# Rows of a few gradient stores moved between DMA engines, in an attention kernel with one query per head

## The chip, the cores and the metric

The kernel runs on one core of a Trainium2 chip. The metric is the time of one execution on the device in microseconds (us). Before the change the median of seven runs is 1286.94 us (1286.24 to 1287.81).

A core has five engines with instruction streams of their own: PE (matrix products), DVE and ACT (elementwise work), POOL, and SP. Here POOL and SP mainly issue DMAs, which 16 DMA engines carry out between the chip's memory (HBM) and the on-chip memory of 128 partitions.

## The reference

For 2 x 32 heads, each with one query row q of 128 numbers and 8192 keys k and values v, all in bf16, it computes attention and its gradients for a given gradient of the output:

```python
scale = q.shape[-1] ** -0.5
scores = jnp.einsum("bhqd,bhkd->bhqk", q, k) * scale
p = _softmax(scores, axis=-1)
out = jnp.einsum("bhqk,bhkd->bhqd", p, v)
_out0, _vjp = jax.vjp(_f, q, k, v)
_grads = _vjp(grad_out)          # dq, dk, dv
```

dk and dv are as large as k and v: 2 MB per head each. With one query row each of them is an outer product: dk is a column of 8192 weights times q, dv a column of 8192 weights times the output's gradient. So 268 MB are read and 268 MB written, and little is computed on each byte.

## The kernel before

The 64 heads are worked on one after the other. A head's k (or v) is one tile of 128 partitions x 64 x 128 numbers, 16 KB in each partition; partition p holds 64 consecutive rows of the sequence, so a partition of the tile is one contiguous run of 16 KB in HBM. Below, "row" means such a partition, and "dv 52" the store of dv of head 52. Twelve tiles (`NTILE`) are held, six heads' worth.

The main loop (`for g in range`) goes through steps of a quarter of a tile (16 of its 64 blocks), eight (`SL`) for a head, and several heads are in it at once, each in another stage: `transpose_chunk` (PE transposes 16 blocks, L184, ACT copies them out, L186), `score_chunk` (PE, L195), the maximum, `expo` and the sums, `acc` (PE sums p v and dS k, L339), and last `outer` (DVE, L394), which overwrites the chunk of the head's own k or v tile with dk or dv. The call of `outer` for the last chunk of a tile also issues its store. `outer` runs v first, then k, so the stores come in the order dv 0, dk 0, dv 1, dk 1 and so on.

A load of head i+6 goes to a tile that head i has left: `slot_of` gives k of head i+6 the tile of v of head i, and v of head i+6 the tile of k of head i. So the load of k of head 58 has to wait until all of dv 52 has landed in HBM, and the load of k of head 61 until all of dv 55 has.

What sets the order of the DMAs:
- `load_eng` is SP: it issues all loads (L98) in the order of the program, each as one DMA of 128 rows. SP also issues the last head's stores, in quarters (L412), and the two small outputs (L489).
- `store_eng` is POOL: it issues the stores (L412, 119 of them) as one DMA of 128 rows each. At the start it also loads 6 rows of q (`FIRST`, L110), behind an instruction (L108) that resets the cursor by which POOL's DMAs are given to DMA engines; the other 58 rows of q are loaded by SP (L114).
- `by_rows` (L87) issues one store as several DMAs, each of some consecutive rows. With `max_dma_last_dim` a row then goes as two runs of 4096 numbers (8 KB). For dk of the heads in `SPREAD` (5, 14, 23, 32, 41, 50, 59) it makes two DMAs, of 126 and of 2 rows.
- `pin` keeps each of these instructions at its place in its engine's program.

The tile framework adds the waits. Each queue's DMAs use eight completion semaphores in turn, so a DMA also waits for the one eight before it on its queue.

Of the kernel before, what the change touches and what calls it, by code (L numbers as in the profile page):

```python
# [17 lines left out]
NG = 2  # L18
NTILE = 12
FIRST = 6  # L20
SPREAD = range(5, 64, 9)


@with_exitstack
def kernel(
# [12 lines left out]
    B, H, Sq, D = q.shape  # L38
    Sk = k.shape[2]
    P = nc.NUM_PARTITIONS  # L40
# [3 lines left out]
    NT = Sk // P  # L44
# [5 lines left out]
    load_eng = nc.sync  # L50
    store_eng = nc.gpsimd
    pin = tc.keep_in_program_order
# [30 lines left out]
    def by_rows(eng, dst, src, rows):  # L83

        p = 0
        for m in rows:
            pin(eng.dma_start(out=dst[p : p + m], in_=src[p : p + m], max_dma_last_dim=NT * D))  # L87
            p += m
# [15 lines left out]
    for w, a in enumerate((q, grad_out)):  # L104
        rows = a.rearrange("b h s d -> (b h s) d")
        r0 = FIRST if w == 0 else 0
        if r0:
# [3 lines left out]
                    out=qd_nat[:r0, w, :], in_=rows[:r0], max_dma_last_dim=D  # L111
# [276 lines left out]
    def outer(i, w, c, ends):  # L388

        h = heads[i]  # L390
        n0 = c * CH
        shape = [P, CH, D // 2, 2]
        pin(
            nc.vector.tensor_tensor(  # L394
                out=h.tile[w][:, n0 : n0 + CH, :].rearrange("p n (e t) -> p n e t", t=2),
                in0=h.qb[w][:]
                .rearrange("p (e t) -> p e t", t=2)
                .unsqueeze(1)
                .to_broadcast(shape),
                in1=h.pair[w][:, n0 : n0 + CH, :].unsqueeze(2).to_broadcast(shape),  # L400
                op=ALU.mult,
            )
        )
        if c + 1 in ends:
            at = ends.index(c + 1)
            b0, b1 = (ends[at - 1] if at else 0) * CH, (c + 1) * CH
            dst = (dv_v if w else dk_v)[i]
            if w == 0 and i in SPREAD:
                by_rows(store_eng, dst, h.tile[w], (P - 2, 2))
            else:  # L410
                eng = load_eng if len(ends) > 1 else store_eng
                pin(eng.dma_start(out=dst[:, b0:b1, :], in_=h.tile[w][:, b0:b1, :]))  # L412
# [10 lines left out]
    for g in range(SL * BH + O0 + NCH + 4 - SL):  # L423
# [15 lines left out]
        if x := within(O1):  # L439
            outer(x[0], 1, x[1], last if x[0] == BH - 1 else whole)  # L440
        if x := within(O0):
            outer(x[0], 0, x[1], last if x[0] == BH - 1 else whole)
        ev = None
        if g < SL * BH:
            i, r = divmod(g, SL)
# [74 lines left out]
```

## Time and profile before

| | |
|---|---|
| median of seven runs | 1286.94 us (1286.24 to 1287.81) |
| the profiled execution: its time | 1286.09 us |
| the profiled execution: span from first to last instruction | 1284.3 us |
| PE, ACT, DVE, POOL busy | 88%, 76%, 73%, 6% of the span |
| HBM read and written | 268.47 MB each, 418 GB/s over the span |
| stores by POOL in one DMA | 119, 66.1 us from issue to landing |
| stores by POOL with `by_rows` | 7 of 126 rows and 7 of 2 rows, 69.6 us |
| loads by SP of a whole tile | 127, 21.2 us from issue to landing |

The profile is of one execution on the chip, and times in it are us from the start of the span. The page gives each engine's busy time, then the span in 40 slices: the line "DMA" has the mean busy share of the 16 DMA engines in each slice in tenths (9 is 90% or more), "GB/s" what they moved. A third part lists the DMA queues: q1 holds what SP issued, q0 what POOL issued, q8 and q14 fetches of instructions; each has its count of packets, MB, and the share of 16 engines' span that its packets took. Other views used: busy times by stretches of the span, an engine's instructions in order of time, and the waits ("A <- B" means that A stood idle until B was done; SPq is SP's queue). Beneath the page lies the trace, which also holds every DMA packet with queue, start, duration and size.

### The profile page before, as it was taken

Reading aid. Unit: us, or ns where it says so; the run is one execution under the profiler, and the core shown is the slowest. Engines: PE = TensorE matmul, PEld = TensorE weight load, DVE = VectorE, ACT = ScalarE, POOL = GpSimd, SP = SyncE. Lnnn points to the kernel's source line nnn. Section 1 sums busy time; section 2 is a strip of 40 time slices with the busy share of each in tenths; the row PEclk is TensorE's granted clock in tenths of the full one; section 3 lists DMA queues with packets and bytes.
Section 4 is the critical chain, followed back from the end, with each engine's and each line's share of the span. In section 5 each row is a group of like instructions: output and inputs, shape, how many; then the busy total and the mean of one; then the engine's idle time right before and its main releaser. Section 6 shows DMA issues by size and latency. Waiting matters only on the chain.

```text
span 1284.3 us, 42575 instructions
## 1 busy us (share of the span) xinstructions
PE 1133.1 (88%) x19268; PEld 860.5 (67%) x19268; DVE 936.4 (73%) x2122; ACT 975.7 (76%) x641; POOL 75.3 (6%) x142
## 2 busy tenths in 40 slices
PE   6999999989898988988889998899888888989880
PEld 5777777666676666766666776677666666667650
DVE  2888888777687777767776776767777777667781
ACT  6888888777787877877777887778777778777750
POOL 0000000000000000000000000000000000000000
PEclk9999999999999999999998998989999999999885
DMA  9999999999999999999999999999999999999996
GB/s 388 425 425 426 427 426 429 427 426 428 426 428 428 427 427 427 416 427 429 428 427 427 425 428 429 427 426 424 427 427 428 428 422 424 428 428 426 421 395 251
DMA packets 39986, 539.68 MB, mean 420 GB/s; under 512 B 5116, under 2 KB 5116, under 8 KB 6396
## 3 DMA queue, kind: packets, MB, share of 16 engines
q1 hardware_dynamic: 20172, 272.70, 49.9%
q0 software_dynamic: 19632, 264.25, 48.8%
q8 instruction: 150, 2.46, 0.7%
q14 instruction: 32, 0.26, 0.0%
HBM read 268.47 MB, written 268.47 MB: 418 GB/s over the span
## 4 chain that ended last, share of the span: by engine, by line
DMA 38%; another core or an unknown queue 30%; PE 17%; DVE 6%; issue 4%; ACT 1%; SPq 1%; POOL 0%; POOLq 0%; DVEq 0%; ACTq 0%
DMA kvt<-in_v_dram 19%; DMA kvt<-in_k_dram 12%; PE tp L184 8%; DMA out_dram<-kvt 7%; PE acc L339 4%; DVE kvt L394 3%; PE sw L195 2%; PE dpw L195 2%; DVE sel L362 1%; ACT ev L186 1%; SPq L98 1%; DMA qd_nat<-in_q_dram 1%; PE dpw L282 0%; DVE sel L356 0%
## 5 line engine op out<-in xcount | busy, mean ns | idle before, releaser
L186 ACT COPY ev<-tp 128x2048 bf16<-128x2048 bf16 x512 | 954.9, 1866 | 265.4 <-PE tp L184 254.5
L184 PE MATMUL tp<-ident_bf,kvt 128*128 128x128 bf16 x8192 | 560.4, 223 | 90.9 <-DMA kvt<-in_v_dram 72.9
L394 DVE TENSOR_TENSOR kvt<-qb,pair 128x2048 bf16<-128x2048 bf16 x512 | 621.6, 1215 | 0.2
L184 PEld LDWEIGHTS <-kvt 128*128 128x128 bf16 x8192 | 491.2, 101 | 97.8 <-DMA kvt<-in_v_dram 76.8
L195 PEld LDWEIGHTS <-ev 128*128 128x128 bf16 x8192 | 243.0, 96 | 209.5 <-issue 153.8
L339 PE MATMUL acc<-kvt,dS_pad 128*64 128x512 bf16 x1024 | 169.9, 415 | 0.9 <-DVE dqT L379 0.9
L339 PE MATMUL acc<-kvt,E_pad 128*64 128x512 bf16 x1024 | 160.5, 394 | 0.0
L195 PE MATMUL dpw<-qdT,ev 128*128 128x1 bf16 x4096 | 140.7, 164 | 16.6 <-DVE qb L177 15.8
L362 DVE SCALAR_TENSOR_TENSOR sel<-acc,diag,sel 128x128 f32<-128x128 f32 x384 | 134.7, 351 | 13.6
L195 PE MATMUL sw<-qdT,ev 128*128 128x1 bf16 x4096 | 142.0, 164 | 1.3 <-ACT ev L186 1.3
L412 POOL DMA_DIRECT2D out_dram<-kvt x119 | 64.0, 537 | 1088.5 <-DVE kvt L394 959.2
L207 DVE TENSOR_REDUCE mp<-sw 128x1 f32<-128x64 f32 x64 | 14.4, 225 | 154.4 <-PE sw L195 154.4
L339 PEld LDWEIGHTS <-dS_pad 128*64 128x64 bf16 x1024 | 37.8, 111 | 25.1 <-issue 6.3
L247 DVE CAST E_pad<-E_f 128x64 bf16<-128x64 f32 x64 | 12.5, 196 | 56.4 <-ACT E_f L238 56.4
L339 PEld LDWEIGHTS <-E_pad 128*64 128x64 bf16 x1024 | 36.4, 108 | 21.3 <-issue 0.7
L376 PE MATMUL acc<-ones,sel 128*128 128x1 f32 x256 | 43.4, 239 | 6.2 <-DVE sel L362 6.2
L282 PE MATMUL dpw<-ld,ones 128*128 128x1 f32 x256 | 46.3, 250 | 0.1
L253 DVE CUSTOM_DVE_ANT_0 junk<-E_f,dpw 128x64 bf16<-128x64 f32 x64 | 14.2, 221 | 41.5 <-PE dpw L195 41.5
L356 DVE TENSOR_SCALAR sel<-acc,diag 128x128 f32<-128x128 f32 x128 | 44.1, 345 | 0.0
L376 PEld LDWEIGHTS acc<-ones,sel 128*128 128x128 f32 x256 | 39.2, 193 | 7.3 <-DVE sel L362 7.3
L177 DVE CAST qb<-dpw 128x128 bf16<-128x128 f32 x128 | 35.5, 278 | 6.0 <-PE dpw L168 6.0
L282 PEld LDWEIGHTS dpw<-ld,ones 128*128 128x128 f32 x256 | 38.2, 188 | 0.5 <-DVE ld L253 0.5
(44 smaller groups left out, 313.5 us busy)
## 6 DMA issues: line engine op xcount, KB each, us to landing
out_dram<-kvt POOLq DMA_DIRECT2D x119, 2048.0 KB, 66.2
kvt<-in_v_dram SPq DMA_DIRECT2D x64, 2048.0 KB, 21.2
kvt<-in_k_dram SPq DMA_DIRECT2D x63, 2048.0 KB, 21.2
out_dram<-kvt POOLq DMA_DIRECT2D x7, 2016.0 KB, 69.3
out_dram<-kvt SPq DMA_DIRECT2D x8, 512.0 KB, 24.2
kvt<-in_k_dram SPq DMA_DIRECT2D x2, 512.0 KB, 4.4
kvt<-in_k_dram SPq DMA_DIRECT2D x1, 1024.0 KB, 7.0
out_dram<-kvt POOLq DMA_DIRECT2D x7, 32.0 KB, 69.8
```

What stands on the lines that cost most here:

```text
L177: pin(nc.vector.tensor_copy(out=h.qb[w][:], in_=h.qbp))
L184: pin(nc.tensor.transpose(tp[:, t, :], src[:, c * CH + t, :], ident_bf[:]))
L186: pin(nc.scalar.copy(out=ev[:], in_=tp[:]))
L195: nc.tensor.matmul(dst[:, c * CH + t : c * CH + t + 1], lhsT=ev[:, t, :], rhs=qdT[:, w, i : i + 1], start=True, stop=True,)
L207: pin(nc.vector.reduce_max(out=h.mp[:], in_=h.s, axis=AX.X))
L282: nc.tensor.matmul(out, lhsT=ones[:].to_broadcast([P, P]), rhs=col, start=True, stop=True)
L339: nc.tensor.matmul(h.acc[w][g : g + CW, :], lhsT=wts[:, n0 : n0 + CW], rhs=rows[:, n0 : n0 + QT, :].rearrange("p n d -> p (n d)"), start=( ...
L356: nc.vector.tensor_scalar(out=h.sel[:], in0=block, scalar1=diag[:, 0:1], scalar2=None, op0=ALU.mult)
L362: nc.vector.scalar_tensor_tensor(out=h.sel[:], in0=block, scalar=diag[:, b : b + 1], in1=h.sel[:], op0=ALU.mult, op1=ALU.add,)
L376: nc.tensor.matmul(h.acc[w][:, 0:1], lhsT=h.sel[:], rhs=ones[:], start=True, stop=True)
L394: nc.vector.tensor_tensor(out=h.tile[w][:, n0 : n0 + CH, :].rearrange("p n (e t) -> p n e t", t=2), in0=h.qb[w][:] .rearrange("p (e t) -> ...
L412: pin(eng.dma_start(out=dst[:, b0:b1, :], in_=h.tile[w][:, b0:b1, :]))
```

## The change

`SPREAD` now ends at 50, so dk 59 is stored like any other head. The stores dv 52 and dv 55 are cut by rows: dv 52 into 9, 95 and 22 rows issued by POOL and the last 2 rows issued by SP; dv 55 into 95 and 33 rows issued by POOL.

```diff
-SPREAD = range(5, 64, 9)
+SHIFT = (52, 55)
+SPREAD = range(5, 52, 9)
...
             dst = (dv_v if w else dk_v)[i]
-            if w == 0 and i in SPREAD:
+            if w == 1 and i == SHIFT[0]:
+                by_rows(store_eng, dst, h.tile[w], (9, 95, 22))
+                pin(load_eng.dma_start(out=dst[P - 2 :], in_=h.tile[w][P - 2 :], max_dma_last_dim=NT * D))
+            elif w == 1 and i in SHIFT:
+                by_rows(store_eng, dst, h.tile[w], (95, 33))
+            elif w == 0 and i in SPREAD:
                 by_rows(store_eng, dst, h.tile[w], (P - 2, 2))
             else:
                 eng = load_eng if len(ends) > 1 else store_eng
```

In SP's program the new store of 2 rows stands behind the load of v of head 57 and ahead of the load of k of head 58. Lines behind the change move by one (`by_rows` is L88) or by six (the stores are L418, loads stay in one line, L99).

## The prediction

> **What bounds the kernel now.** I read the page from the top: busy shares, then the slices.
>
> ```profile
> PE 1133.1 (88%) x19268; PEld 860.5 (67%) x19268; DVE 936.4 (73%) x2122; ACT 975.7 (76%) x641; POOL 75.3 (6%) x142
> ...
> DMA  9999999999999999999999999999999999999996
> GB/s 388 425 425 426 427 426 429 427 426 428 426 428 428 427 427 427 416 427 429 428 427 427 425 428 429 427 426 424 427 427 428 428 422 424 428 428 426 421 395 251
> ...
> q1 hardware_dynamic: 20172, 272.70, 49.9%
> q0 software_dynamic: 19632, 264.25, 48.8%
> q8 instruction: 150, 2.46, 0.7%
> q14 instruction: 32, 0.26, 0.0%
> ```
>
> No compute engine is full; the 16 DMA engines are, in every slice but the last. Loads run on q1, POOL's stores on q0, instruction fetches on q8 and q14. So the tail decides. The view of stretches shows it (busy time of each engine, then granted clock, DMA share, GB/s):
>
> ```profile
> 1246.00:1258.00 12.00, 5.93 (x25) 2.41 (x21) 11.24 (x20) 0.00 (x0) 0.00 (x0) 0.50 1.01 419
> 1258.00:1262.00 4.00, 0.44 (x2) 0.17 (x2) 0.57 (x3) 0.00 (x0) 0.00 (x0) 0.50 0.91 375
> 1262.00:1265.00 3.00, 0.00 (x0) 0.00 (x0) 0.00 (x0) 0.00 (x0) 0.00 (x0) 0.50 0.71 298
> 1265.00:1272.00 7.00, 0.00 (x0) 0.00 (x0) 0.00 (x0) 0.00 (x0) 0.00 (x0) 0.50 0.57 238
> 1272.00:1273.00 1.00, 0.00 (x0) 0.00 (x0) 0.00 (x0) 0.00 (x0) 0.00 (x0) 0.50 0.45 184
> 1273.00:1279.00 6.00, 0.00 (x0) 0.00 (x0) 0.00 (x0) 0.00 (x0) 0.00 (x0) 0.50 0.43 180
> 1279.00:1281.00 2.00, 0.00 (x0) 0.00 (x0) 0.00 (x0) 0.00 (x0) 0.00 (x0) 0.50 0.36 143
> ```
>
> Compute ends at 1259.4 us; what follows is the draining of stores. A share of 0.57 is 9 engines of 16, 0.43 is 7. Seven DMA engines end early, two at about 1272.5, seven between 1280 and 1282.3; the span ends 2.07 us behind the last of them. The end belongs to the DMA engine with the most work, since none runs dry before the tail.
>
> **Which engine is which.** The trace lists each DMA packet with queue, start, duration and size, not its engine. On one engine a packet starts 3 to 4 ns before the last one's end, so the packets can be strung into 16 chains. Small transfers name them: the six rows of q that POOL loads mark six engines (0 to 5), the 58 rows that SP loads lie as 29 and 29 on two of these (0 and 1), and the seven dk stores spread now give 14 chains 9 rows each and two of the six 1 row each (4 and 5). Last data of each chain, without idle time spent waiting for the very last small store:
> - seven of engines 6 to 14: 1280.0 to 1282.25. Each carries 18 or 19 packets of q8, about 1.0 us each.
> - engine 4 or 5, the slow one (a 16 KB packet every 629 ns, all others 607): 1272.5. The other: 1252.2.
> - engines 0 and 1: 1255.8 and 1264.9.
> - engines 2 and 3: 1262.1 and **1272.6**. The latter, X, carries 18 packets of q14, and its 16 KB packets took 616.5 ns in the mean, the other's 613.4.
> - three more without q8, one of them engine 15: 1256.8, 1261.1 and 1265.4.
>
> These ends give the 9 and 7 of the stretches.
>
> **The change, part by part.** It moves rows of 16 KB between engines; the bytes stay. A row costs 0.607 us as one packet, and 2 x 0.306 us in the stores by rows, where it goes as two of 8 KB. In the trace a store of 126 rows takes 14 engines from a cursor, 9 consecutive rows each, and 2 rows the next two; 6 rows took six. Carried on (the row count's largest divisor up to 16, the cursor behind the last engine): 9 rows to engines 6-14, 95 to 15 and 0-3 with 19 each, 22 and 33 to 4-14 with 2 and 3 each. SP's two rows go to 0 and 1, as its 58 rows did.
>
> [...]
>
> Rows over dk of head 59 and dv of 52 and 55, before and after:
> - engines 6-14: 9+8+8 = 25, then 8+3+3 = 14. In packets: 6 x 0.306 + 8 x 0.607 = **6.7 us less**. Ends 1273.3 to 1275.6.
> - engines 4, 5: 1+8+8, then 8+2+3: 8 x 0.607 - 8 x 0.306 = 2.4 less (slow one 2.5). Ends 1270.0 and 1249.8.
> - engines 15, 2, 3: 25, then 8+19+19 = 46: 58 x 0.306 - 8 x 0.607 = **12.9 more**. [...] I take 13.4, since part of X's slow packets belong to fetches, not to rows.
> - engines 0, 1: one row more, 47: 13.5 more. Ends 1269.3 and 1278.4.
>
> So engine 15 ends by 1278.3 at most, the lighter of 2 and 3 at 1275.0, and **X at 1272.6 + 13.4 = 1286.0** (1285.5 to 1286.8), past the 1282.25 that ends the kernel now. The seven that were late lose 6.7 us and are no longer the bound, but X takes their place 3.8 us later. Rows were taken from the right engines and put on one that had only 9.7 us to spare.
>
> **Waits added.** DVE, PE and ACT get none. POOL issues four more DMAs (L87's rows: 0.69 us each, POOL busy 6%): hidden. But each POOL store also waits, by the program's eight store semaphores in turn, until the one eight before it has landed: 97.0 us now, 11 times. With three DMAs for dv 52, dv 55 has to wait for its first part, which landed at 1102, where POOL issued dv 55 at 1089.5: 13 us late. Five stores are queued then, at some 10 us each: covered.
>
> SP's new store has its place behind the load of head 57's v and ahead of that of head 58's k, and SP works in order:
>
> ```profile
> 1092.60 0.33 SPq L98 DMA_DIRECT2D kvt<-in_v_dram  x1
> 1102.24 0.33 SPq L98 DMA_DIRECT2D kvt<-in_k_dram  x1
> ...
> SPq L98 <- DMA out_dram<-kvt: 1137.5, 116, 24.3
> ```
>
> SP waits 1137.5 us for landed stores: each load waits for the store that frees its tile. The 1092.60 line is head 57's v; POOL issued dv 52 at 1036.5, and head 58's k went out at 1102.24 when it had landed. Now two rows of dv 52 leave at 1093 and land 4.4 us later (the shortest load on the page) or 21.2 (the usual one), behind head 57's v: 1097 to 1114. Head 58's k is 0 to 12 us late; I take 10, as the queue is full then. PE waits for that k, up to 10 us, and wins back some 2 us a head (88% busy). From head 61's k on, dv 55 lands on X some 4 us later than on the last engine now, 8 where stores and loads take turns, or 13 by POOL's wait. Compute may so end up to 18 us late, at 1277. X's POOL stores last until 1265.3 now, 1278 then, and SP's final stores (10 us of packets) follow; X stays fed, and I cost these waits at nothing. With that cover gone they would show, at up to 8 us (18 less the 10 of the last stores). A gain from them is excluded: nothing is released earlier than its store on X.
>
> **Sum.** X's last data 1286.0 + 2.07 = span 1288.1, against 1284.3: +3.8. The profiled execution took 1286.09 (span + 1.8), so 1289.9; it is 0.85 below the median of the seven runs, 1286.94. Whether X shares that 0.85, which may belong to the seven late engines alone, is unknown; I take half: **1290.3**.
>
> **Rivals.**
> 1. *X is not among the five.* For it: chains cross thousands of times, and a swap in the first 60 us would misname them. Against it: 18 q14 packets stay on one chain, and that chain has a row of q from POOL. Then the latest are engine 0 or 1 at 1278.4 and 15 at 1278.3: span 1280.5, 3.8 less: 1282.3, by the median 1283.1. This is the faster end, 0.17.
> 2. *The row counts do not pick the engines this way* (95 rows on all 16). Then dk 59 alone changes, the late seven lose one row, 0.6 us: 1286.3. Chance 0.05.
> 3. *The waits of SP and POOL are not covered.* Slower: decided where compute ends more than 19 us late, or stores of heads 58 to 61 are held until X's q0 runs dry. 3.8 and up to 8 on top: 1294 to 1298. For it: SP's single file. Against it: 66 us of queued stores. Chance 0.10.
> 4. *My forecast*, X last: 0.68, 1289.0 to 1291.6.
>
> **Chances and range.** A measurement of this kernel can tell some 0.2%, 2.6 us, from no change; same means 1284.4 to 1289.5. Of the forecast about three quarters lie above 1289.5 (0.51), the rest within; rival 3 adds 0.09 to slower; rival 1 gives faster 0.15 and 0.02 within; rival 2 is within. Slower 0.60, same 0.25, faster 0.15. The range reaches from rival 1 to the lower part of rival 3: 1283.0 to 1295.0. For slower cases alone: 1289.0 to 1295.0.
>
> **What would show it.** Right: in the tail the DMA share falls to about 0.06 (one engine) for the last 6 to 8 us, where now seven share the end; the span grows by 3 to 5; compute ends 5 to 18 us later; head 58's k leaves SP about 10 us after its place. Wrong: a tail in which many engines end together by 1280 (X misnamed); an unchanged 0.43 up to 1279 (rows spread over all 16); full DMA share broken by gaps ahead of 1250 (rival 3).

## The result, and the profile after

The changed kernel takes 1294.28 us (median of 12 runs, 1291.57 to 1298.35), the kernel before 1287.58 us in the same comparison (30 runs, 1285.96 to 1291.96). The ratio is 1.0053, with a 95% interval of 1.0044 to 1.0062: slower by 6.7 us. 1290.3 had been forecast, in a range of 1283.0 to 1295.0; against the 1286.94 from which the forecast started that is a loss of 3.4 us. The profiled execution took 1295.20 us, its span is 1293.4 us (1284.3 before).

The page shows where the time is lost. The sums for the queues stay as they were but for the cut rows; three slices fall to 389 to 410 GB/s, and the last is emptier:

```profile
DMA  9999999999999999999999999999999999999995
GB/s 388 423 428 427 426 427 426 428 428 428 426 428 426 428 428 426 422 426 428 429 427 423 425 427 429 427 424 425 429 427 426 427 410 393 389 421 416 427 410 213
```

The dip lies in slices 33 to 35 (1035 to 1132 us), where cut stores are on their way; the DMA engines are called busy there as everywhere. Next, the stretches of the changed kernel (busy time of PE, weight load, DVE, ACT and POOL, then granted clock, DMA share, GB/s):

```profile
1000.00:1200.00 200.00, 171.46 (x2867) 130.12 (x2865) 138.88 (x315) 145.04 (x97) 13.94 (x23) 0.92 1.00 410
...
1246.00:1258.00 12.00, 10.22 (x154) 6.97 (x150) 10.35 (x26) 6.86 (x6) 0.53 (x1) 1.00 0.91 386
...
1265.00:1272.00 7.00, 2.06 (x10) 0.76 (x4) 4.93 (x11) 0.00 (x0) 0.00 (x0) 0.50 1.00 412
1272.00:1273.00 1.00, 0.00 (x0) 0.00 (x0) 0.00 (x0) 0.00 (x0) 0.00 (x0) 0.50 0.84 343
1273.00:1279.00 6.00, 0.00 (x0) 0.00 (x0) 0.00 (x0) 0.00 (x0) 0.00 (x0) 0.50 0.61 249
1279.00:1281.00 2.00, 0.00 (x0) 0.00 (x0) 0.00 (x0) 0.00 (x0) 0.00 (x0) 0.50 0.22 90
1281.00:1284.00 3.00, 0.00 (x0) 0.00 (x0) 0.00 (x0) 0.00 (x0) 0.00 (x0) 0.50 0.12 49
1284.00:1286.00 2.00, 0.00 (x0) 0.00 (x0) 0.00 (x0) 0.00 (x0) 0.00 (x0) 0.50 0.07 31
1286.00:1288.00 2.00, 0.00 (x0) 0.00 (x0) 0.00 (x0) 0.00 (x0) 0.00 (x0) 0.50 0.06 23
1288.00:1290.00 2.00, 0.00 (x0) 0.00 (x0) 0.00 (x0) 0.00 (x0) 0.00 (x0) 0.50 0.06 27
```

Where seven engines shared the end before, now one is left alone from 1284 us on: a share of 0.06 is one engine of 16. Compute is done at 1271 us, 12 us later than before, and the engines are still full then (1.00). The same packets strung into 16 chains give the last data of each engine:

| engine | before | forecast | after |
|---|---|---|---|
| X (of 2 and 3; 18 or 19 fetches on q14) | 1272.6 | 1286.0 | 1291.7 |
| the other of 2 and 3 | 1262.1 | 1275.0 | 1276.9 |
| 0 and 1 | 1255.8, 1264.9 | 1269.3, 1278.4 | 1274.5, 1281.2 |
| 15 | not told apart | at most 1278.3 | 1278.1 |
| the seven late ones of 6 to 14 | 1280.0 to 1282.3 | 1273.3 to 1275.6 | 1275.9 to 1283.5 |
| 4 or 5, the slow one | 1272.5 | 1270.0 | 1273.3 |

On five chains the two cut stores show as 76 half rows (38 rows) on the 95-row part: 2 x 19 rows each. X is one of the five.

SP's instructions in order of time show the waits: v of head 57, the two rows of dv 52, k of head 58, and further down k of head 61.

```profile
1097.28 0.33 SPq L99 DMA_DIRECT2D kvt<-in_v_dram  x1
1097.70 0.73 SPq L411 DMA_DIRECT2D out_dram<-kvt  x1
1115.86 0.35 SPq L99 DMA_DIRECT2D kvt<-in_k_dram  x1
...
1150.04 0.33 SPq L99 DMA_DIRECT2D kvt<-in_v_dram  x1
1177.53 0.33 SPq L99 DMA_DIRECT2D kvt<-in_k_dram  x1
```

Head 58's k left at 1102.24 before, so it is 13.6 us late. Head 61's k is 15.5 us late; before, it left here:

```profile
1161.99 0.33 SPq L98 DMA_DIRECT2D kvt<-in_k_dram  x1
```

POOL's two issues of dv 55, which had its place at 1089.53, are the two lines of L88 here:

```profile
1100.28 1.02 POOL L88 DMA_DIRECT2D out_dram<-kvt  x1 [2.07 <-DVE sel L357]
1109.03 0.62 POOL L88 DMA_DIRECT2D out_dram<-kvt  x1 [7.73 <-DMA out_dram<-kvt]
```

They are 10.8 and 19.5 us late. And one thing stands in no line above: a packet of 16 KB takes 611 ns on most engines, one of 8 KB 309 ns, but between 1120 and 1140 us POOL's packets of 16 KB took 728 ns in the mean and its packets of 8 KB 507. Below, **excess** is the sum, over all data packets of 16 and 8 KB that started between 1020 and 1260 us, of the time beyond these 611 and 309 ns. It is 59 us of engine time before, half of it around the cut dk 59, and 129 us after.

### The profile page after: what moved, and what is told of

Its sections match the earlier page's. It is cut to its first block, busy times and chain, and to the rows that moved or that the text cites. A ratio compares the mean times of both kernels' runs of the same rounds, so it can differ in the third digit from the quotient of the medians.

```text
span 1293.4 us, 42582 instructions
## 1 busy us (share of the span) xinstructions
PE 1127.1 (87%) x19268; PEld 857.2 (66%) x19268; DVE 936.1 (72%) x2122; ACT 975.7 (75%) x641; POOL 77.4 (6%) x144
## 4 chain that ended last, share of the span: by engine, by line
another core or an unknown queue 34%; DMA 33%; PE 18%; DVE 7%; issue 4%; ACT 1%; SPq 1%; POOL 0%; POOLq 0%; DVEq 0%; ACTq 0%
DMA kvt<-in_k_dram 15%; DMA kvt<-in_v_dram 14%; PE tp L185 8%; PE acc L340 5%; DVE kvt L395 4%; DMA out_dram<-kvt 3%; PE sw L196 2%; PE dpw L196 2%; DVE sel L363 1%; ACT ev L187 1%; SPq L99 1%; DMA qd_nat<-in_q_dram 1%; PE dpw L283 1%; DVE sel L357 0%
## 5 line engine op out<-in xcount | busy, mean ns | idle before, releaser
L363 DVE SCALAR_TENSOR_TENSOR sel<-acc,diag,sel 128x128 f32<-128x128 f32 x384 | 134.7, 351 | 13.6
L418 POOL DMA_DIRECT2D out_dram<-kvt x118 | 63.5, 538 | 1074.9 <-DVE kvt L395 950.4
```

Of the source, the lines that this page charges most:

```text
L363: nc.vector.scalar_tensor_tensor(out=h.sel[:], in0=block, scalar=diag[:, b : b + 1], in1=h.sel[:], op0=ALU.mult, op1=ALU.add,)
```

## The experiments

All start from the changed kernel, so dk 59 is whole unless it is told otherwise. Ratios are to the kernel before, whose median was 1288.2 to 1288.7 us beside them. In the first eight and the last two the two branches for dv are one, with POOL issuing all parts:

```diff
-            if w == 1 and i == SHIFT[0]:
-                by_rows(store_eng, dst, h.tile[w], (9, 95, 22))
-                pin(load_eng.dma_start(out=dst[P - 2 :], in_=h.tile[w][P - 2 :], max_dma_last_dim=NT * D))
-            elif w == 1 and i in SHIFT:
-                by_rows(store_eng, dst, h.tile[w], (95, 33))
+            if w == 1 and i in SHIFT:
+                by_rows(store_eng, dst, h.tile[w], SHIFT[i])
```

**The 95 rows on other engines.** The parts ahead of the 95 rows are changed, so that these begin at engine 13 and go to 13, 14, 15, 0 and 1.

```diff
+SHIFT = {52: (7, 95, 26), 55: (14, 95, 13, 6)}
```

> dv 52 goes as 7+95+26 rows and dv 55 as 14+95+13+6, all by POOL, so that the 95 rows fall on engines 13, 14, 15, 0 and 1 and engine X (2 or 3, with the 18 fetches on q14) gets 13 rows over the three stores where the changed kernel gives it 46. Theory X (the end is the work of engine X): X ends early, the last is one of the new five, at 1265.4 + 24 rows (14.7) = 1280.1, plus the 5.6 us by which X ended later than its row count in the changed kernel if those fall on any five engines: 4 to 10 us faster than the changed kernel, ratio to the kernel before 0.998 to 1.003. Theory W (the waits of loads for stores cut by rows): as many pieces and as uneven, so as slow as the changed kernel, ratio about 1.005.

Measured: 1309.12 us, ratio 1.0171 (1.0146 to 1.0196). I had taken 13 and 14 for engines with time to spare. They are not: in the fourth kernel, which puts 95 rows on the same five, two of the chains with the 95-row part carry 17 and 18 fetches on q8, so 13 and 14 belong to the seven late ones. Two engines are all that is left from 1290 to 1302 (a share of 0.12 to 0.15), as they must be if the most loaded engines end the kernel. The waits show here too, on the other engines. POOL stood idle for 24.06 us, until 1119.40, for a landed store; head 61's k left SP at 1193.02, 31 us later than before; DVE worked until 1288; and most DMA engines ran dry ahead of the tail:

```profile
1266.00:1270.00 4.00, 3.68 (x62) 2.69 (x64) 2.71 (x7) 3.37 (x4) 0.00 (x0) 1.00 0.58 246
1270.00:1274.00 4.00, 2.70 (x32) 1.45 (x30) 3.86 (x11) 0.58 (x1) 0.53 (x1) 0.99 0.41 172
```

So with seven parts the waits of rival 3 are no longer covered on these engines. In the chains the two that end last have no such gap, so it is their load that sets the end; but the run doesn't test X as I had meant.

**SP's store given to POOL.**

```diff
+SHIFT = {52: (9, 95, 24), 55: (15, 95, 18)}
```

> dv 52 as 9+95+24 rows, dv 55 as 15+95+18, all by POOL: the five engines 15 and 0 to 3 as in the changed kernel, X with 47 rows for 46, but SP issues no store. Theory X: as slow as the changed kernel, 0.6 us more for X's row, ratio 1.005 to 1.006. Theory W with SP's single file as the cause: the load of head 58's k no longer waits behind SP's store, and most of the loss goes, ratio 1.000 to 1.003.

Measured: 1300.17 us, 1.0097 (1.0077 to 1.0117). Head 58's k leaves SP at 1109.55 here, 6.3 us earlier than in the change, and the kernel is slower, not faster. So there is no sign that SP's single file is what the change costs; but dv 55 is also in three parts here instead of two, and that can hide a small gain. At the end three engines are left, and then one:

```profile
1284.00:1286.00 2.00, 0.00 (x0) 0.00 (x0) 0.00 (x0) 0.00 (x0) 0.00 (x0) 0.50 0.18 75
1286.00:1290.00 4.00, 0.00 (x0) 0.00 (x0) 0.00 (x0) 0.00 (x0) 0.00 (x0) 0.50 0.08 32
1290.00:1294.00 4.00, 0.00 (x0) 0.00 (x0) 0.00 (x0) 0.00 (x0) 0.00 (x0) 0.50 0.06 26
```

**Only dv 55 cut, on the five engines of the change.**

```diff
+SHIFT = {55: (9, 95, 24)}
```

> Only dv 55 is cut (9+95+24 rows), dv 52 is whole, dk 59 whole. Theory X: X gets 35 rows for 25, ends at 1272.6 + 6.1 to 6.9 = 1279; engines 6 to 12 lose 6 rows, 3.7 us, and end at 1278.6: 3 us faster than before by row counts, equal to before if half of the 5.6 us beyond the row count comes with one cut store: ratio 0.997 to 1.000. Theory W: half the loss of the changed kernel, ratio 1.002 to 1.003.

Measured: 1284.84 us, 0.9966 (0.9951 to 0.9981), faster than before. The chains: X ends at 1277.4, the seven late ones at 1276.4 to 1279.3, engine 15 at 1263.7. With half of the extra rows X has caught up with the seven and not passed them. Many engines end together:

```profile
1270.00:1274.00 4.00, 0.00 (x0) 0.00 (x0) 0.00 (x0) 0.00 (x0) 0.00 (x0) 0.50 0.61 251
1274.00:1278.00 4.00, 0.00 (x0) 0.00 (x0) 0.00 (x0) 0.00 (x0) 0.00 (x0) 0.50 0.43 171
1278.00:1280.00 2.00, 0.00 (x0) 0.00 (x0) 0.00 (x0) 0.00 (x0) 0.00 (x0) 0.50 0.04 15
```

**Only dv 55 cut, on engines 13, 14, 15, 0 and 1.**

```diff
+SHIFT = {55: (7, 95, 26)}
```

> Only dv 55 is cut, as 7+95+26 rows: the 95 on engines 13, 14, 15, 0 and 1. Theory X: engines 6 to 12 lose 6 rows and end at 1278.6, the five at 1272.8 at the latest, X loses 7 rows: 3.7 us faster than before by row counts, 1 us with the extra of one cut store: ratio 0.997 to 0.999. Theory W: half the loss of the changed kernel, ratio 1.002 to 1.003.

Measured: 1297.78 us, 1.0075 (1.0055 to 1.0095). The same number of parts and of bytes as in the kernel before it, and nearly the same excess (73 against 59 us), but the rows lie on two of the late engines: 1.1% slower. This pair is the test of the row count as a cause that the first kernel was meant to be. Two engines are left alone:

```profile
1282.00:1284.00 2.00, 0.00 (x0) 0.00 (x0) 0.00 (x0) 0.00 (x0) 0.00 (x0) 0.50 0.11 45
1284.00:1286.00 2.00, 0.00 (x0) 0.00 (x0) 0.00 (x0) 0.00 (x0) 0.00 (x0) 0.50 0.14 59
1286.00:1290.00 4.00, 0.00 (x0) 0.00 (x0) 0.00 (x0) 0.00 (x0) 0.00 (x0) 0.50 0.12 49
```

**Only dk 59 whole, no store of dv cut.**

```diff
+SHIFT = {}
```

> Only dk 59 is stored whole; dv 52 and dv 55 are whole as before. By row counts: engines 6 to 15 and 0 to 3 lose one row (0.6 us), engine 4 gains 7 rows (4.4 us) and ends at 1276.9, ahead of the last at 1281.7. Theory X (the most loaded DMA engine ends last): ratio 0.999 to 1.000. Theory C (packets are slowed wherever a store is cut, so each cut store has a price of its own): the cut of dk 59 is gone as well, so up to 2 us faster, 0.998 to 0.9995.

Measured: 1284.21 us, 0.9969 (0.9958 to 0.9981), beyond what I had expected of it. This smallest part of the change is worth 4.0 us (1288.23 less 1284.21), where its rows are worth 0.6. The excess falls from 59 to 28 us: around the cut dk 59 the 8 KB packets of before take 342 to 400 ns in the mean (309 without a disturbance), and here nothing is cut. What the changed kernel loses, it loses against this one: 1.0053 to 0.9969, a factor of 1.0084 or 10.8 us for the two cuts of dv.

**Both stores cut in even parts.** 64, 48 and 16 rows, and twice 64. By the divisor that 126, 95, 58, 6 and 2 rows followed, an estimate, each part goes to all 16 engines in equal shares (4, 3 and 1 rows): no engine gets more than its 8 rows. Which rows it gets the traces don't tell.

```diff
+SHIFT = {52: (64, 48, 16), 55: (64, 64)}
```

> dk 59 whole; dv 52 as 64+48+16 rows and dv 55 as 64+64, which gives every DMA engine 8 rows of each store, but in pieces, as 8 KB packets, and other rows than the whole store gives it. Five DMAs where the changed kernel has five by POOL and one by SP. Theory X (unequal rows): like dk 59 alone, 0.999 to 1.000, and packets of 8 KB at 309 to 325 ns in the mean. Theory C with the pieces and the exchanged rows as the cause of slow packets: half or more of the 5.6 us that X lost beyond its row count shows here on all engines, ratio 1.002 to 1.005. Theory W (POOL's and SP's waits for more and smaller stores): the same, from loads that leave SP 5 to 15 us late.

Measured: 1289.48 us, 1.0007 (0.9991 to 1.0023). Against the kernel with dk 59 alone this is 0.38%, 4.9 us, though by that estimate every engine keeps its number of rows. So the cuts of these two stores have a price of their own, beside that of the rows. The excess is 89 us.

**Only dv 52 cut.**

```diff
+SHIFT = {52: (9, 95, 24)}
```

> Only dv 52 is cut, as 9+95+24 rows (the five 15 and 0 to 3). Theory X: like dv 55 alone, which was 0.9966: X ends near 1277.4, engines 6 to 12 at 1276 to 1280, ratio 0.996 to 0.998. Theory C: the slow packets come by chance of how the cut store meets the other traffic, so it may differ from dv 55 alone by some us either way; above 0.999 would speak for it.

Measured: 1287.12 us, 0.9991 (0.9979 to 1.0002); the excess is 78 us. That is 2.8 us more than with dk 59 alone, where the cut of dv 55 cost nothing. Each cut alone costs 2.8 us or less, both cost 10.8: as long as X has time to spare its extra rows are free, and the second cut finds too little left. Rows are not all of it: X's 1277.4 with dv 55 alone and 6.8 us of rows for the second cut make 1284.2, and X ended at 1291.7 in the change.

**The two cuts farther apart.** dv 60 in place of dv 55.

```diff
+SHIFT = {52: (9, 95, 24), 60: (15, 95, 18)}
```

> The two cut stores of e2 (9+95+24 and 15+95+18 rows, X with 47 rows), but dv 52 and dv 60 in place of dv 52 and dv 55, so that the first has long landed when the second begins. Theory X with slow packets from two cut stores that overlap: X ends at 1272.6 + 13.5 + about 2, span 1290, ratio 1.004 to 1.006, faster than e2 (1.0097) by 5 us. Theory that each cut store has its own slow packets: as e2, 1.008 to 1.011.

Measured: 1303.72 us, 1.0119 (1.0101 to 1.0137). So the loss needs no overlap of the cut stores. The overlap does add slow packets: the excess is 118 us here and 161 us with the same parts of dv 52 and dv 55 in the second kernel, while dv 55 alone adds 31 us and dv 52 alone 50 us to the 28 us of no cut. One engine is left alone for 16 us:

```profile
1286.00:1290.00 4.00, 0.00 (x0) 0.00 (x0) 0.00 (x0) 0.00 (x0) 0.00 (x0) 0.50 0.06 27
1290.00:1294.00 4.00, 0.00 (x0) 0.00 (x0) 0.00 (x0) 0.00 (x0) 0.00 (x0) 0.50 0.07 30
1294.00:1298.00 4.00, 0.00 (x0) 0.00 (x0) 0.00 (x0) 0.00 (x0) 0.00 (x0) 0.50 0.06 26
```

**The change without its edit of dk 59.**

```diff
-SPREAD = range(5, 52, 9)
+SPREAD = range(5, 64, 9)
```

> The change without its edit of dk 59: dv 52 and dv 55 are cut as in the changed kernel, and dk 59 is cut into 126 and 2 rows as before. Theory A (the end is the last data of the most loaded DMA engine, and every cut store has a price of its own of some 3 to 5 us, because packets are slowed while its pieces are on their way): dk 59 whole gained 4 us when it was the only edit, so it is given back, 1298 us, about 1.0085 of before. Theory B (dk 59 whole gained only because it relieved the seven late engines, which no longer end the kernel here): only rows count, 9 of half size instead of 8 whole ones on the engine X, +0.6 us: 1294.9, about 1.0057. Theory D (the prices of cuts do not add, since the slow packets of one cut run beside others): between the two or under 1294.

Measured: 1303.13 us, 1.0100 (1.0084 to 1.0116). To leave dk 59 whole is worth 0.47%, 6 us, here too, where X ends the kernel and rows account for 0.6 us of it. It is not only the seven late engines that it helps. The excess is 158 us.

**The parts of the change as plain DMAs.** Without the bound on a run's length a row is one packet of 16 KB.

```diff
-                by_rows(store_eng, dst, h.tile[w], (9, 95, 22))
+                by_rows(store_eng, dst, h.tile[w], (9, 95, 22), None)
...
-                by_rows(store_eng, dst, h.tile[w], (95, 33))
+                by_rows(store_eng, dst, h.tile[w], (95, 33), None)
```

Here `by_rows` leaves out `max_dma_last_dim` where its new last argument is None.

> The changed kernel with the same pieces of dv 52 and dv 55 from POOL (9, 95 and 22 rows; 95 and 33 rows), but as plain DMAs without the bound on a run's length, so that a row goes as one packet of 16 KB where nothing else splits it; SP's two rows stay as they are. Theory A1 (the rows stay on the same engines by the divisor rule, and the halving of the rows is what slows packets): X has the 46 rows still and no excess beyond 3 us, 1286.0 + 2.1 + 1.8 = 1290 or a little less, about 1.002. Theory A2 (the rows stay, and it is the uneven shares that slow packets): 1294, about 1.005. Theory A3 (plain DMAs of POOL go to all 16 engines whatever the row count, 6 rows an engine or fewer): no engine is loaded beyond the others, the end is that of dk 59 alone plus what the pieces cost, 1284 to 1287, 0.997 to 1.000, and the tail ends with many engines together. Packets of 8 KB on POOL's queue after 1030 us would then be only those of dk 50 and of none later.

Measured: 1291.29 us, 1.0021 (1.0009 to 1.0033). Most chains carry 1, 6 and 2 rows for dv 52 and 6 and 3 for dv 55, some the sixes alone: in this form 95 rows go to all 16 engines, 6 to one. By rows, in the change, they went to five. The most loaded engines have 18 rows of the two stores, where whole stores give 16: 1.2 us. The last data comes from several engines together:

```profile
1278.00:1280.00 2.00, 0.00 (x0) 0.00 (x0) 0.00 (x0) 0.00 (x0) 0.00 (x0) 0.50 0.50 202
1280.00:1282.00 2.00, 0.00 (x0) 0.00 (x0) 0.00 (x0) 0.00 (x0) 0.00 (x0) 0.50 0.36 142
1282.00:1284.00 2.00, 0.00 (x0) 0.00 (x0) 0.00 (x0) 0.00 (x0) 0.00 (x0) 0.50 0.17 67
```

Still the time is 0.5% (6.7 us) above that of dk 59 alone, more than I had allowed, with an excess of 99 us and no halved row in the two stores but the two that SP stores. So packets get slow without halving.

**Two plain halves.** dv 52 and dv 55 in two plain DMAs of 64 rows.

```diff
+SHIFT = {52: (64, 64), 55: (64, 64)}
...
+                by_rows(store_eng, dst, h.tile[w], SHIFT[i], None)
```

> dk 59 whole; dv 52 and dv 55 from POOL in two plain DMAs of 64 rows each (whole 16 KB packets, the same rows for every engine if POOL's plain DMAs go to all 16 engines). Against the kernel with dk 59 whole and no cut (1284.2 us, 0.9969 of before). Theory N (it is the number of DMAs that a store is cut into that slows packets, whatever their shape): two extra DMAs, 2 to 6 us more, 0.9985 to 1.0015, and packets on the two big queues take 30 us or more of engine time beyond their usual 611 ns between 1080 and 1160. Theory S (it is unequal shares, which put the engines out of step): the shares are equal here, so nothing is added: 0.996 to 0.998, no excess beyond some 15 us.

Measured: 1301.86 us, 1.0088 (1.0066 to 1.0110), 1.2% above dk 59 alone. The chains carry 4 rows of each half. So the shares are equal, nothing is halved, the cut adds only two DMAs, and the price is the highest of all cuts in equal shares: I had expected 6 us at most. The excess is 172 us. The dip in the rates is the longest seen (slices 33 to 38), and two engines go on alone for some 13 us:

```profile
GB/s 388 424 427 427 425 426 427 428 428 428 425 427 428 427 428 421 417 428 426 429 427 426 426 428 427 428 426 425 427 429 427 424 420 393 410 395 395 415 373 187
```

```profile
1284.00:1286.00 2.00, 0.00 (x0) 0.00 (x0) 0.00 (x0) 0.00 (x0) 0.00 (x0) 0.50 0.19 79
1286.00:1290.00 4.00, 0.00 (x0) 0.00 (x0) 0.00 (x0) 0.00 (x0) 0.00 (x0) 0.50 0.14 60
1290.00:1294.00 4.00, 0.00 (x0) 0.00 (x0) 0.00 (x0) 0.00 (x0) 0.00 (x0) 0.50 0.12 49
1294.00:1298.00 4.00, 0.00 (x0) 0.00 (x0) 0.00 (x0) 0.00 (x0) 0.00 (x0) 0.50 0.13 51
```

**Cut in the form of dk 50.**

```diff
+SHIFT = {52: (126, 2), 55: (126, 2)}
```

> dk 59 whole; dv 52 and dv 55 cut by rows into 126 and 2 rows, the form that dk 50 has in every kernel here (where the trace of before shows no slowed packets behind it: 3.2 us of excess between 1060 and 1080). Rows alone: 9 of two halves instead of 8 whole ones, twice, 1.3 us more on the fourteen engines, so 0.998 of before. Theory F (this form of cut costs nothing, only more pieces or other shares do): 0.997 to 0.999. Theory L (a cut costs by its place, because it releases a tile that a load near the end waits for): 4 to 8 us more, 1.000 to 1.003, with slowed packets behind 1080.

Measured: 1287.93 us, 0.9993 (0.9983 to 1.0004), 0.24% above dk 59 alone; 1.3 of these 3.1 us are rows. The excess is 71 us, 29 of it between 1080 and 1120. The ratio lies between the ranges of the two theories, and its interval reaches into both. The form that slows next to no packets at dk 50 slows many at dv 52 and 55. Nor is dk 50 alone in this: every kernel here has six cuts of this form, dk 5 to dk 50. In the trace of before some 2 us of excess is usual in a stretch of 20 us, and the highest stretch around them has 2 to 3 us at dk 5, 14 and 32, 9 at dk 23, 6 at dk 41 and 5 at dk 50, but 19 at dk 59. So the form of a cut does not set its price. What is different at the late ones is not shown.

All kernels beside each other, by their excess:

| kernel | ratio | excess, us |
|---|---|---|
| dk 59 whole, nothing cut | 0.9969 | 28 |
| before (dk 59 cut) | 1 | 59 |
| dv 55 cut | 0.9966 | 59 |
| 126 and 2 rows twice | 0.9993 | 71 |
| dv 55 cut, on late engines | 1.0075 | 73 |
| dv 52 cut | 0.9991 | 78 |
| even parts | 1.0007 | 89 |
| plain parts | 1.0021 | 99 |
| dv 52 and dv 60 cut | 1.0119 | 118 |
| **the change** | 1.0053 | 129 |
| 95 rows on other engines | 1.0171 | 154 |
| the change and dk 59 cut | 1.0100 | 158 |
| the change without SP's store | 1.0097 | 161 |
| plain halves | 1.0088 | 172 |

The excess is that of one profiled execution each, the ratio that of medians. The kernels in which no engine has more than 18 rows of the two stores, for 16 in whole ones (dk 59 alone, 126 and 2, even parts, plain parts, plain halves), stand in the order of their excess. Their profiled executions do so too, but for even parts (1293.03 us) and plain parts (1287.93), which change places. Dearest for their excess are dv 55 on late engines, dv 52 and 60, and 95 rows on other engines: there one or two engines got more rows than they had time for.

## Why the prediction was right, and where it was not

**What bounds the kernel.** Right. The end is the last data of the DMA engine with the most work, plus some 2 us: X's 1291.7 and a span of 1293.4 here, 1279.3 and 1281.4 with dv 55 alone.

**Which engines get which rows.** Right. The divisor with a cursor gave the five engines, 38 rows on each. The counts that the traces show fit it: 126 rows on 14 engines, 58 on two, 6 on six and 2 on two before, 95 on five in the change. That the rows on one engine are consecutive is not shown, the traces tell only how many there are; the forecast needs no more. What rival 2 supposed, 95 rows on all 16, happens with plain DMAs, 6 rows on an engine.

**X as the new bound.** Right: X ends 8 us after the next engine, at a share of 0.06. Rival 1 is out. With dv 55 alone X ends at 1277.4, level with the seven; the second cut, which the forecast's own prices put at 19 x 0.612 - 8 x 0.607 = 6.8 us, makes X the last by rows alone (1284.2), and with slow packets it ends at 1291.7.

**What a row costs X: the step that was mis-sized.** "X at 1272.6 + 13.4 = 1286.0" was 19.1 in place of 13.4. The rows themselves are the 12.9 that had been counted. Between 1030 and 1230 us the data packets of X take 11.3 us beyond 611 and 309 ns, 3.2 before: 8.1 more. 12.9 + 8.1 is 21.0, 1.9 above the 19.1; excess that X had before around dk 59 behind 1230 us is not in the 3.2, and I can't place the remainder more closely. The forecast took each row at its undisturbed time, 12.9 in all, and 0.5 on top (1.3 at the top of its range). No run shows these; in their place the trace after shows the 8.1 us of slow packets. While the parts of a cut store are on their way packets are slower on the seven as well as on X: between 1060 and 1140 us POOL's packets of 16 KB took 663 ns in the mean (618 before) and those of 8 KB 387 (316).

**The gain of the seven.** "6.7 us less, ends 1273.3 to 1275.6" came out as 1275.9 to 1283.5, for the same reason: their excess between 1030 and 1230 rose from 1.1 to 1.4 us each to 3.9 to 9.5.

**dk 59 whole.** Counted as a row's worth in that sum (0.6 us for the seven); alone it gained 4.0 us, and 6 us within the change. The slow packets around dk 59 stood in the trace of before (8 KB packets at 342 to 400 ns from 1200 us on, 309 to 333 around dk 50), and I had not looked for them. This error and that on the two cuts have opposite signs, and it is luck that 1290.3 came as near as 4 us. Of the loss itself, 6.7 us, the forecast had half, 3.4.

**Waits.** Put at nothing, and nothing they cost the end. Head 58's k was 13.6 us late (10 taken, 12 at most), head 61's 15.5 (4 to 13), compute 12 (up to 18, 1277). X had no idle time from 900 to 1235 us, so the cover held. Rival 3, whose time of 1294 to 1298 is the one measured, is not what happened: its mark, gaps ahead of 1250, is in the trace (0.91 from 1246 to 1258), but on engines that don't end the kernel, and X, which does, was never idle. Even in the first experiment, where the waits do empty most engines (a share of 0.41), the two that end last keep working.

**Why packets get slow** is narrowed down, not settled. None of these is needed for it: SP's store (kernels without it have slow packets too), the overlap of the two stores (each cut alone has them, though the overlap adds to them), halved rows (plain parts have almost none), unequal shares (plain halves have the highest excess). Nor is it the small packets of 4 bytes: there are 868 more of them on POOL's queue, at 9 ns each, and X has 0.1 us of them more. What else a cut changes is not shown: the traces tell how many rows an engine moves, not which, nor from where to where a packet goes. In the plain halves between 1080 and 1180 us, 75 of 1293 16 KB packets of POOL took 1200 ns or more (half of them 1.4 us or more, the longest 4.0 us), and 1 of 1316 where nothing is cut. What held them up the trace doesn't tell. That a part has 64 rows doesn't set the price: even parts also have halves of 64 rows, and their excess around dv 55 is smaller (6, 6, 3 and 14 us in the four stretches of 20 us from 1100 on; 15, 17, 21 and 28 with plain halves). And the six early cuts, dk 5 to dk 50, show little excess, 2 to 9 us in the highest stretch of 20 us around each.

**A version that beats both** came out of it: dk 59 whole and nothing else, 0.9969 of before; with dv 55 alone cut, on the five engines of the change, 0.9966, the same within the intervals.

## What to carry to other kernels

When all DMA engines are full, count the load of each engine by itself, with the instruction fetches that only some of them carry (here 18 or 19 of about 1 us on each of eight engines): moving rows helps only until the engine that gets them becomes the last. Don't price rows of a store that is cut at the time of rows in a whole store without looking at the packet durations around the cuts that the kernel already has, near the place where the new one goes: here six early cuts show few slow packets, and the late ones slowed packets of both big queues while they were on their way (16 KB packets between 1080 and 1120 us: 636 ns in the mean for loads and 639 for stores, 614 and 620 before the change). And take a change of several edits apart: here its smallest edit alone was a gain, and the two others cost more than that.

## What the runs showed of the hardware that I had not expected

- The same DMA of 95 rows goes to 5 engines (19 rows each) when its rows are split in two runs, and to all 16 (6 rows on an engine) when it is left plain.
- Two stores of 2 MB in two plain halves each, with as many rows on each engine as whole, cost 15.3 us (1.0088 to 0.9969, of 1288), with 75 of 1293 packets at twice their usual time or more. Cut into 126 and 2 rows they cost 3.1 us.
- The 16 engines are far from alike over this kernel: the 150 fetches of about 1 us on q8 come on eight of them, 18 or 19 on each (the seven late ones and one more), X carries 18 or 19 on q14, and one of 4 and 5 takes 632 ns in the mean for a 16 KB packet where most take 611.
